# A fused linear-attention and FFN kernel on one Trainium2 core: another order of the same steps, with the front's large loads on SP's queue and other shares of DVE and ACT

## The chip, the cores and the metric

The kernel runs on one core of one Trainium2 chip. The metric is the device time of one execution in microseconds (us); the time before is 149.65 us, the median of three runs (149.62 to 149.75). The engines are named as in the profile: PE does the matrix products (PEld is its weight load), DVE, ACT and POOL work on vectors, and SP only issues transfers. ACT can issue transfers too. Each engine runs its own instruction list strictly in order, and engines wait for each other by semaphores.

## The reference

The input is one sequence of 2048 rows of 448 columns. The rows are normalised once, and two branches work on the result: an attention of 16 heads of 28 columns with a softmax feature map, and a two-layer FFN with a Mish activation. The output is the input plus both branches.

```
xn  = (x - mean) / sqrt(var + 1e-5)                     # per row
q, k, v = split heads of xn @ wqkv                      # 16 heads of 28
pq, pk  = q @ w_phi[h], k @ w_phi[h]
phi = concat(softmax(p), softmax(-p))                   # 56 features, for q and for k
kv, z   = sum_s phi_k x v, sum_s phi_k
o   = (phi_q @ kv) / (phi_q @ z + 1e-6)
A   = o @ wo
h   = xn @ w1 + b1;  B = (h * tanh(softplus(h))) @ w2   # Mish, 1792 wide
out = x + A + B
```

## The kernel before

The 2048 rows are 16 tiles t of 128 rows, or 8 pairs u of two tiles. The whole program is a list of named steps (ORDER, lines 181 to 198). `run_order` (L201) calls them one after the other; each step appends its instructions to the lists of the engines that it uses, and a resource tracker (class Program, L40) adds the semaphore waits that the data need. So the place of a name in ORDER sets its place on each engine that it uses, transfers included, and nothing else: two steps on different engines are ordered by data alone.

The names are built from a step, a tile, pair or part, and a last letter that says which engine does it: s SP, a ACT, d DVE, p POOL, m an SP transfer, b both ACT and DVE.

- **Loads.** `lx0` to `lx6` load rows of x (L307; lx0, lx1, lx2, lx3 two tiles each, from tile 0, 2, 4, 6; lx4 and lx6 four tiles each, from 8 and 12). `lkm` and `lvm` load the first 384 rows of the K and V weights into the tile Wkv (L310), `lkt` their last 64 rows twice, into both halves of the partitions (L315; `lktb` issues one copy on SP and one on ACT, `lkts` both on SP). `lp` is w_phi (tile Wraw, L330), `lb` is b1 (L334), `lqT0` to `lqT3` are transposing loads of the Q weight (L319), `l1m` and `l1t` load W1, `l2` W2, `lo` Wo. `table` loads ACT's function table (L348).
- **Row normalisation.** `st` computes mean and variance of one tile (two DVE instructions, L471 and L472, or five on ACT, L463 to L467). `rs` and `rt` compute 1/sqrt for a pair or for one tile (two on ACT, L483 and L485, or two on POOL, L477 and L480). `xn` and `xm` apply both (DVE L512, or after a shift on DVE, L490, on ACT L507 or on POOL L502). Pair 1 alone (tiles 2 and 3) goes by single tiles: `rt2`, `rt3`, `xm2`, `xm3`.
- **Transposes of the normalised rows** into xnT: `xt` for a pair, `xh` for one tile of pair 1. With a or d they go through PE (L520, L536) and are copied out by that engine (L527 or L525); with m they are an SP transfer (L546).
- **Folded weights.** `wtk0`, `wtk1` transpose the K weight on PE (L585) and copy it out; `bdp` builds the block-diagonal w_phi on POOL (tile Wbd, L568); `wmk0`, `wmk1` multiply the two (L609) into Wpk, `wmq0`, `wmq1` the same for Q into Wpq. `qd` (DVE, L323) doubles 64 columns of the transposed Q weight and needs all four `lqT`.
- **Products** (L433): `k`, `q`, `v` of a pair u and `f` of the FFN's first layer (f0.c and f1.c: half of the rows, column block c). Each product fills one of four pairs of PSUM banks and is cut in three parts, A, H and B, of 6, 2 and 6 matmuls of 64 partitions; two of these run at once, on the two halves of the array. The bank pair is taken at the first part and comes free when the evacuation is done: two exponentials on ACT for k (L650) and q (L712), a copy on ACT or DVE for v (L525 or L527), a Mish on ACT for f (L731).
- **The features of k.** `kn` sums over the features on DVE (L658, L660) and scales on POOL (L662), twice per pair u. `kv` accumulates phi_k times v on PE (L681), eight in all; `kvz` copies the sum out on DVE (L692) and turns it by an SP transfer (L698).
- **The end.** `e` turns the exponentials of q by an SP transfer (L720); `nd` forms numerator and denominator of a tile on PE (L754) and divides on DVE (L770 to L781), `ot` turns the result by an SP transfer (L789), `wo` multiplies by Wo (L877), `g` is the FFN's second layer (L860), the sum is added to x on DVE (L824) and stored (`sto`, L891). The last tile's last 64 columns come separately (L839 to L846, store L888).
- **Warm-up.** `z5` and `z6` are 5 and 6 matmuls on zeros (L402) at the head of PE's list; `b1` turns the bias on PE (L725) and DVE copies it out.

Four matters of this listing carry the steps below. PE's list begins z5, z6, b1, wtk0b, wtk1b, xh3d, xh2a, xt3a, wmk0a, wmk1b, and then the products. The copy of the K weight's tail that SP issues stands behind x's tiles 2, 3, 6 and 7 and w_phi. The engines' lists are in order, so a DVE instruction that waits holds all rows behind it. And the parts B and A of one product wait for each other on PE, so other products stand between them.

Of the kernel before, what the change touches and what calls it, by code (L numbers as in the profile page):

```python
# [178 lines left out]


ORDER = """
zero lx1s lx3s lba st2d lkma lps pw pp st6d lktb lx2s table z5 pi lvma st3a z6 pm lx4s rt3a st7d rs3a xm3a lqT0 rt2p
xm2d b1 xn3d wtk0b bdp wtk1b xh3d st5d xh2a st4d lqT2 xt3a wmk0a wmk1b lqT3 rs2p v1Aa lqT1 st8d v1Ha v3Bd lx6s st9a
v1Ba pk v3Hd k3B xn2d v3Ad rs4p qd k3H xt2m xn4d k3A st14d st15d st12d rs7p lx0s st11d k1H k1A wmq0a wmq1a k1B v2Bd
st13d k2A rs6a k2H v2Ad xn7p st10d q1H xt4m l1ms k2B xn6p v2Hd q1A q2B q1B q2H st1d st0d xt7m q2A e2 v4Ad rs5a v4Hd
k4A v4Bd k4H xn5d q3B k4B q3H q3A xt6m rs0p q4A v7Ha ep xn0d v7Aa kn2.0 xt5m kn4.0 e3 xt0m l1ts k7B v7Ba k7A k7H k6A
k6H pv kn3.0 v6Bd k6B q4B k5B v6Hd kn1.0 v6Ad k5H q4H v5Hd kn4.1 v5Ad k5A k0B kn7.1 v5Bd k0A k0H f0.1H kn3.1 f0.1A
f1.2A kn7.0 kn1.1 kn0.0 f0.1B f1.3H f1.3A f1.2H f0.0B f1.3B e9 e4 f1.0A kn2.1 f1.0H f0.0H kn6.0 f0.0A e7 f1.0B f1.2B
q7H e8 kn0.1 q7A q5A v0Hd q7B e5 e6 q5H v0Bd q6A los v0Ad q6H q5B q6B f1.9B kv3 kn5.1 kv4 kv7 e11 f0.7A f1.9H f1.9A
f0.7H f0.13A e10 f0.13H kv1 kv0 f0.13B e12 f0.7B e13 kn6.1 f1.13A f1.13H q0B f1.13B q0H f0.6H kn5.0 kv2 kv6 kv5 kvz  # L190
q0A f0.6A e1 f0.9H f0.9A f1.10A f1.10H f0.6B f0.2B f1.10B f0.2A f0.9B e14 f1.12A f0.2H e0 f1.11A f1.12H f0.5A f1.11H
nd1 f1.12B f1.11B f0.5B f1.8A f0.5H l2s nd2 f1.8H f0.8B f1.8B f0.10A nd3 ot1m f0.10H f0.8H f0.8A f1.5A f0.10B e15
f1.5B f1.1B nd0 f0.12H f1.1H f1.1A f0.12B f1.5H f0.3H f0.3A nd7 f0.3B f0.12A f1.7A ot0m f0.11B f1.7H f1.4B nd6 f1.7B
f1.4H ot3m f0.11H f1.4A f0.11A wo1H f0.4B f1.6B f0.4H f0.4A f1.6H nd10 f1.6A wo1B nd4 wo1A nd5 wob nd11 g3 g0 g2 ot2m
g1 nd13 wo3H wo3A wo0B nd12 ot5m wo3B wo0H ot6m nd14 sto1 wo0A g7 g6 g10 g11 nd8 wo5B nd15 ot7m wo5H nd9 wo5A sto3
wo2A g4 g5 g13 g12 ot4m g8 wo4B wo6H wo7A wo2H wo6A wo4H wo2B wo7B sto0 wo6B sto6 sto5 wo4A wo7H g9 g14 sto4 stt14
sto2 g15 stt15
"""


# [822 lines left out]
```

## Time and profile before

| | |
|---|---|
| median of three runs | 149.65 us |
| the profiled execution's own time | 149.63 us |
| its span in the trace | 147.4 us |
| PE busy | 143.1 us, 97% |
| DVE, ACT, POOL busy | 101.8, 77.0, 39.4 us |

The span is what the profiler sees from the first to the last instruction; the time of the execution lies 2.2 us above it. PE is busy in nearly all of the span: of the 40 slices of the page, the first two have 70%, the last 30%, and the others 90% or more. The chain of waits gives PE 93% of the span, DMA 4%, SP's queue and DVE 1% each. ACT is busy until 90 us, POOL until 56 us, DVE until the end.

### The profile page before, as it was taken

Reading aid. Unit: us, or ns where it says so; the run is one execution under the profiler, and the core shown is the slowest. Engines: PE = TensorE matmul, PEld = TensorE weight load, DVE = VectorE, ACT = ScalarE, POOL = GpSimd, SP = SyncE. Lnnn points to the kernel's source line nnn. Section 1 sums busy time; section 2 is a strip of 40 time slices with the busy share of each in tenths; the row PEclk is TensorE's granted clock in tenths of the full one; section 3 lists DMA queues with packets and bytes.
Section 4 is the critical chain, followed back from the end, with each engine's and each line's share of the span. In section 5 each row is a group of like instructions: output and inputs, shape, how many; then the busy total and the mean of one; then the engine's idle time right before and its main releaser. Section 6 shows DMA issues by size and latency. Waiting matters only on the chain.

```text
span 147.4 us, 3868 instructions
## 1 busy us (share of the span) xinstructions
PE 143.1 (97%) x1668; PEld 74.1 (50%) x1668; DVE 101.8 (69%) x227; ACT 77.0 (52%) x98; POOL 39.4 (27%) x54
## 2 busy tenths in 40 slices
PE   7799999999999999999999999999999999999993
PEld 2275555554445545444544446555555545547452
DVE  0898996989997921306999848998997499303522
ACT  3999999989889987996667575000000000000000
POOL 6334283399999990000000000000000000000000
PEclk9999999999999999999999999999999999999999
DMA  4995899995998195399707311015032004500313
GB/s 133 296 274 169 156 350 112 198 202 79 157 203 224 26 163 112 61 190 242 232 4 133 67 32 35 0 24 99 8 57 67 0 4 104 145 0 0 129 64 122
DMA packets 39964, 17.23 MB, mean 117 GB/s; under 512 B 33932, under 2 KB 39180, under 8 KB 39948
## 3 DMA queue, kind: packets, MB, share of 16 engines
q1 hardware_dynamic: 38896, 16.09, 51.3%
q10 hardware_dynamic: 1052, 0.91, 2.1%
q8 instruction: 13, 0.21, 0.6%
q14 instruction: 3, 0.02, 0.0%
HBM read 7.02 MB, written 1.84 MB: 60 GB/s over the span
## 4 chain that ended last, share of the span: by engine, by line
PE 93%; DMA 4%; SPq 1%; DVE 1%; issue 0%
PE PS L433 51%; PE PS L860 29%; PE PS L877 7%; DMA Wkv<-in_A_wqkv_dram 4%; PE PS L754 3%; PE PS L681 2%; PE PS L609 1%; SPq L307 1%; PE PS L585 0%; DVE x_all L824 0%; SPq L330 0%; PE PS L536 0%; PE PS L520 0%; DVE x_all L846 0%
## 5 line engine op out<-in xcount | busy, mean ns | idle before, releaser
L433 PE MATMUL PS<-xnT,W 64*128 64x512 bf16 x392 | 44.8, 376 | 0.0
L860 PE MATMUL PS<-W,actT 128*128 128x448 bf16 (+1 forms) x224 | 42.7, 351 | 0.0
L731 ACT ACTIVATE actT<-PS,b1T 128x1024 bf16<-128x1024 f32 x28 | 30.0, 1113 | 9.3 <-PE PS L433 9.2
L860 PEld LDWEIGHTS PS<-W,actT 128*128 128x128 bf16 x224 | 21.6, 98 | 20.6 <-issue 1.1
L433 PEld LDWEIGHTS PS<-xnT,W 64*128 64x128 bf16 x392 | 18.3, 94 | 21.0 <-issue 0.3
L662 POOL TENSOR_TENSOR actT<-actT,rSk 128x896 bf16<-128x896 bf16 x16 | 26.6, 1700 | 4.8 <-DVE rSk L660 4.8
L824 DVE TENSOR_TENSOR x_all<-PS,x_all 128x448 bf16<-128x448 f32 (+1 forms) x16 | 9.1, 614 | 13.9 <-PE PS L877 8.5
L658 DVE TENSOR_REDUCE Sk<-actT 128x32 f32<-128x896 bf16 x16 | 16.6, 1040 | 0.0
L650 ACT ACTIVATE actT<-PS 128x896 bf16<-128x896 f32 x16 | 13.8, 932 | 0.3 <-PE PS L433 0.2
L433 PE MATMUL PS<-Wkv,xnT 64*128 64x448 bf16 x112 | 13.2, 349 | 0.0
L770 DVE COPY Sq<-PS 128x16 f32<-128x16 f32 x32 | 4.0, 168 | 13.2 <-PE PS L754 13.2
L433 PE MATMUL PS<-Wpk,xnT 64*128 64x448 bf16 x112 | 13.1, 349 | 0.0
L433 PE MATMUL PS<-Wpq,xnT 64*128 64x448 bf16 x112 | 12.7, 349 | 0.0
L471 DVE BATCH_NORM_STATS2 stats<-x_all 128x6 f32<-128x448 bf16 x14 | 8.5, 606 | 3.5 <-DMA x_all<-in_A_x_dram 3.5
L778 DVE TENSOR_TENSOR v_all<-v_all 128x464 f32<-128x464 f32 x16 | 10.3, 643 | 0.6
L774 DVE TENSOR_TENSOR v_all<-PS,Sq 128x464 f32<-128x464 f32 x16 | 10.3, 641 | 0.5
L781 DVE TENSOR_TENSOR xn<-v_all,rden 128x448 bf16<-128x448 f32 x16 | 10.0, 625 | 0.6
L776 DVE TENSOR_TENSOR v_all<-PS,Sq 128x464 f32<-128x464 f32 x16 | 10.1, 630 | 0.0
L712 ACT ACTIVATE actT<-PS 128x896 bf16<-128x896 f32 x10 | 8.4, 925 | 0.6 <-PE PS L433 0.5
L527 DVE CAST v_all<-PS 128x896 bf16<-128x896 f32 x6 | 6.5, 1080 | 3.0 <-PE PS L433 3.0
L433 PEld LDWEIGHTS PS<-Wkv,xnT 64*128 64x128 bf16 x112 | 5.4, 94 | 5.0
L433 PEld LDWEIGHTS PS<-Wpq,xnT 64*128 64x128 bf16 x112 | 5.4, 94 | 5.1 <-ACT actT L731 0.2
(85 smaller groups left out, 121.0 us busy)
## 6 DMA issues: line engine op xcount, KB each, us to landing
W<-in_B_w_dram SPq DMA_DIRECT2D x1, 1568.0 KB, 8.2
out_dram<-x_all SPq DMA_DIRECT2D x7, 224.0 KB, 2.2
W<-in_B_w_dram SPq DMA_DIRECT2D x1, 1344.0 KB, 6.8
x_all<-in_A_x_dram SPq DMA_DIRECT2D x4, 224.0 KB, 2.9
x_all<-in_A_x_dram SPq DMA_DIRECT2D x2, 448.0 KB, 5.1
Wkv<-in_A_wqkv_dram ACTq DMA_DIRECT2D x2, 336.0 KB, 5.1
Wo<-in_A_wo_dram SPq DMA_DIRECT2D x2, 336.0 KB, 4.3
W<-in_B_w_dram SPq DMA_DIRECT2D x2, 224.0 KB, 3.6
```

Of the source, the lines that this page charges most:

```text
L433: ins = e.matmul(o, lhs(c, k), rhs(c, k), start=first and n == at[par][0], stop=last and n == at[par][-1])
L650: op("ACT", lambda e, s=s: e.activation(E_of(u)[:, s, :, :], two(b, D), ACT.Exp, scale=1.0 if s == 0 else -1.0), r=[pb(b), pb(b + 1)], w=[ ...
L658: op("DVE", lambda e: e.tensor_reduce(Sk[u][:, s, :], Eh(), AX.X, ALU.add), r=[("E", u, s)], w=[("Sk", u, s)], tag=f"Sk{u}.{s}")
L662: op("POOL", lambda e: e.tensor_tensor(Eh(), Eh(), ap_on(rSk[u][:, s, 0:1], [[1, 2 * H], [0, DH]]), ALU.mult), r=[("E", u, s), ("rSk", u, ...
L731: op("ACT", lambda e: e.activation(actT[:, fc, q * 1024:(q + 1) * 1024], bank(b, 2), ACT.Mish, bias=b1T[:, fc:fc + 1]), r=[("b1T",), pb(b) ...
L774: op("DVE", lambda e: e.tensor_tensor(tv(t1[i]), num(0), sx(1), ALU.mult), r=[pb(b), pb(b + 1), ("Sq", i, 1)], w=[("t1", i)], tag=f"ta{t}")
L776: op("DVE", lambda e: e.tensor_tensor(tv(t2), num(1), sx(0), ALU.mult), r=[pb(b), pb(b + 1), ("Sq", i, 0)], w=[("t2",)], tag=f"tb{t}")
L778: op("DVE", lambda e: e.tensor_tensor(t1[i], t1[i], t2, ALU.add), r=[("t1", i), ("t2",)], w=[("t1", i)], tag=f"tc{t}")
L781: op("DVE", lambda e: e.tensor_tensor(o_sb[(t // 2) % 2][:, t % 2, :].rearrange("p (h d) -> p h d", d=DH), t1[i][:, :, 0:DH], ap_on(rden[i ...
L824: op("DVE", lambda e: e.tensor_tensor(x_all[:, t, 0:n], bank(b)[:, 0:n], x_all[:, t, 0:n], ALU.add), r=[pb(b), ("x", t)], w=[("out", t)], ...
L860: ins = e.matmul(bank(b)[:, 0:width(t)], actT[:, fc, tok(t)], W2[:, fc, 0:width(t)], start=first and fc == 0, stop=last and fc == FC - 1)
L877: ins = e.matmul(bank(b)[:, 0:w], oT_of(u)[lo:hi, cc * P:(cc + 1) * P], Wo[lo:hi, cc, 0:w], start=first and n == at[par][0], stop=last and ...
```

## The change

Only ORDER changes; no function does. The new list has as many steps as the old, and 30 of them carry another letter or count. In words:

- **Loads.** `lkma`, `lktb`, `lvma` become `lkms`, `lkts`, `lvms`: the K and V weights are issued on SP. SP's list now begins lx3, lx1, lp, lkm, lkt (two copies), lx2, lvm, lx4, lx6, lqT0, lqT3, lqT1, lqT2, xt2m, lx0, l1m, xt4m, xt5m, xt7m, xt0m, xt6m, l1t (two). Before it began lx1, lx3, lp, lkt (one copy), lx2, lx4, lqT0, lqT2, lqT3, lqT1, lx6, xt2m, lx0, xt4m, l1m, xt7m. ACT's list begins with `table`, and then the one small load lb.
- **First rows.** Statistics: tiles 7, 3, 2 on DVE and tile 6 on ACT (before: 2, 6, 7 on DVE, 3 on ACT). `rs3`, `rt2`, `rt3` all on ACT (before, rt2 on POOL). `xn3`, `xm2`, `xm3` all on DVE (before, xm3 on ACT with its shift on DVE). `xh2` and `xh3` both copied out by DVE (before, xh2 by ACT). `wtk1` copied out by ACT alone (before by both), `wmk0` by both (before by ACT), `wmq0` by DVE (before by ACT).
- **Later rows.** `st9` on DVE and `st11` on ACT (before the other way round); `rs5` and `rs6` on POOL (before on ACT); `xn7` on DVE (before on POOL). v2, v3, v4 and v0 are copied out by ACT (before by DVE). `pv`, a memset on POOL, moves ahead of the `kn` rows, `pk` behind them.
- **Warm-up.** z10, b1, z4 in place of z5, z6, b1: 14 matmuls on zeros, four of them behind b1.
- **Order of the products.** After v1, v3, k1, k3 come k2, v2, q1, q2, q3, k4, v4, k5, v5, k7, k0, v0, v7, k6, four f, then q5, q4, v6, q6. The `kv` steps stand earlier, the `nd` steps begin with nd3, nd2, and the list ends g8, g9, g5, g4, g15 (before wo4A, wo7H, g9, g14, g15).

```diff
--- before.py
+++ after.py
@@ -179,22 +179,21 @@
 ORDER = """
-zero lx1s lx3s lba st2d lkma lps pw pp st6d lktb lx2s table z5 pi lvma st3a z6 pm lx4s rt3a st7d rs3a xm3a lqT0 rt2p
-xm2d b1 xn3d wtk0b bdp wtk1b xh3d st5d xh2a st4d lqT2 xt3a wmk0a wmk1b lqT3 rs2p v1Aa lqT1 st8d v1Ha v3Bd lx6s st9a
-v1Ba pk v3Hd k3B xn2d v3Ad rs4p qd k3H xt2m xn4d k3A st14d st15d st12d rs7p lx0s st11d k1H k1A wmq0a wmq1a k1B v2Bd
-st13d k2A rs6a k2H v2Ad xn7p st10d q1H xt4m l1ms k2B xn6p v2Hd q1A q2B q1B q2H st1d st0d xt7m q2A e2 v4Ad rs5a v4Hd
-k4A v4Bd k4H xn5d q3B k4B q3H q3A xt6m rs0p q4A v7Ha ep xn0d v7Aa kn2.0 xt5m kn4.0 e3 xt0m l1ts k7B v7Ba k7A k7H k6A
-k6H pv kn3.0 v6Bd k6B q4B k5B v6Hd kn1.0 v6Ad k5H q4H v5Hd kn4.1 v5Ad k5A k0B kn7.1 v5Bd k0A k0H f0.1H kn3.1 f0.1A
...
-f1.5B f1.1B nd0 f0.12H f1.1H f1.1A f0.12B f1.5H f0.3H f0.3A nd7 f0.3B f0.12A f1.7A ot0m f0.11B f1.7H f1.4B nd6 f1.7B
-f1.4H ot3m f0.11H f1.4A f0.11A wo1H f0.4B f1.6B f0.4H f0.4A f1.6H nd10 f1.6A wo1B nd4 wo1A nd5 wob nd11 g3 g0 g2 ot2m
-g1 nd13 wo3H wo3A wo0B nd12 ot5m wo3B wo0H ot6m nd14 sto1 wo0A g7 g6 g10 g11 nd8 wo5B nd15 ot7m wo5H nd9 wo5A sto3
-wo2A g4 g5 g13 g12 ot4m g8 wo4B wo6H wo7A wo2H wo6A wo4H wo2B wo7B sto0 wo6B sto6 sto5 wo4A wo7H g9 g14 sto4 stt14
-sto2 g15 stt15
+zero table lx3s lba pi st7d st6a lx1s pp st3d lps st2d rs3a rt2a z10 pw rt3a lkms lkts lx2s pm b1 xn3d lvms xm2d lx4s
+xm3d z4 wtk0b bdp wtk1a xh2d xh3d st4d st5d xt3a wmk0b lx6s wmk1b rs2p v1Ha lqT0 v3Ba lqT3 v1Ba st11a lqT1 xn2d v3Aa
+v3Ha k3H k1B lqT2 v1Aa st8d xt2m ep st9d k1H k1A qd st10d k3A wmq0d rs4p wmq1a pv k3B k2A k2H lx0s st15d l1ms v2Ha q1B
+xn4d k2B st14d rs5p rs7p st1d q1H v2Ba q1A xt4m q2H xn5d v2Aa xn7d q3H q2A xt5m q3A q2B st0d st12d q3B k4B xt7m v4Ba
+rs0p k4A st13d k4H rs6p k5B xn0d xn6p v4Aa xt0m kn1.1 k5H xt6m v5Ad kn2.1 v4Ha v5Hd k5A kn3.1 v5Bd k7H k7A k0B k7B
+v0Ba v7Ha k0H l1ts v0Ha k0A v7Ba k6B e2 e5 v7Aa k6H kn4.1 k6A f1.2A v0Aa f1.2H f1.3B f1.2B kn3.0 los f1.0A f0.1A f1.0H
+kn4.0 e3 f0.1H kn0.1 kn5.1 f1.3H kn1.0 kn5.0 f1.3A kn7.1 f0.1B e6 q5B kn2.0 f1.0B e4 q4B v6Bd q4A v6Hd kn6.1 e7 q4H
+q6B v6Ad q5A q5H q6A kv1 kv3 q6H f1.7B f1.11A kn0.0 e8 f1.7A kn6.0 f1.11H f1.7H f0.7B kv5 kv2 kv4 f1.11B kn7.0 f0.7A
+f1.9B f0.7H f0.10B kv6 kv0 kv7 f1.9H pk e13 kvz f1.9A e12 f0.6H f0.10A f0.10H f0.6A f0.0B f0.6B f0.0H f0.0A q7A e9 q0A
+q0H q7H e10 nd3 q0B f1.12B e0 q7B f1.12H f1.8H f1.8A e11 nd2 f1.8B f1.12A f0.13A f0.13H f1.10B f0.13B f1.10A f0.8A
+ot1m f1.10H f1.5B nd6 f0.8H f1.5A e1 f0.3H f1.5H f0.3A f0.8B nd7 e15 f0.5B f0.3B f0.5H f0.11B f0.5A nd0 f1.6H f1.6A
...
+f1.4H f0.4B f1.4B f0.9B f0.4H f0.12B nd13 f0.4A f0.9H f0.9A wo0B nd11 wo0A wo0H nd12 nd10 ot6m g1 g0 g12 g13 nd5 wo1H
+wo1A wo6H wo6A ot5m nd4 wo1B nd15 wo6B g2 g6 ot2m g3 wo3H nd9 sto6 nd14 wo3B nd8 wo3A g7 ot7m g10 ot4m g11 g14 wo2A
+wo4H wo7B sto3 wob wo4B wo5H wo2H wo7A wo4A wo5B wo2B wo7H sto0 sto1 wo5A g8 g9 sto4 g5 g4 stt14 sto5 sto2 g15 stt15
 """
```

More of the change, by code (lines that the diff above doesn't have):

```diff
@@ L187 @@
-k6H pv kn3.0 v6Bd k6B q4B k5B v6Hd kn1.0 v6Ad k5H q4H v5Hd kn4.1 v5Ad k5A k0B kn7.1 v5Bd k0A k0H f0.1H kn3.1 f0.1A
[L188 to L191, printed above, removed]
```

2 lines of the change are left out of this document (1 added, 1 removed).

## The prediction

> **What bounds the kernel now.** I read the page's shares first, then the chain of waits in order of time (start, length, what).
>
> ```profile
> PE 143.1 (97%) x1668; PEld 74.1 (50%) x1668; DVE 101.8 (69%) x227; ACT 77.0 (52%) x98; POOL 39.4 (27%) x54
> ```
>
> ```profile
> 2.20 5.20 DMA Wkv<-in_A_wqkv_dram
> ...
> 7.44 0.65 PE PS L585 x8
> 8.10 0.39 PE PS L536 x7
> 8.49 0.39 PE PS L520 x7
> 8.88 0.79 PE PS L609 x16
> 9.67 4.84 PE PS L433 x50
> 14.50 0.89 PE PS L609 x16
> 15.40 34.03 PE PS L433 x348
> ...
> 57.50 0.88 PE PS L681 x96
> ...
> 144.45 0.56 DVE x_all L824
> ```
>
> The reader is to see three stretches. Until 7.40 the chain is the second copy of the K weight's tail, issued by SP at 2.20. Until 9.67 it is PE with little rows in a fixed order. From 9.67 to 144.4 it is PE alone. The same matmuls are done after the change, and both lists end with g15, its DVE sum and the stores, so the 2.97 us from 144.43 to the span's end stay, and the 2.23 us between span (147.4) and time (149.63) too. What can change is **when the products start**, and **whether PE, in its new order, is ever made to wait**. The profiled run stands 0.02 under the median of 149.65; I count against the median, with 0.2% (0.3 us) as what a measurement can tell from no change.
>
> **The front: loads.** The timeline of the first microseconds (start, length, engine, line):
>
> ```profile
> 0.82 0.87 SPq L307 DMA_DIRECT2D x_all<-in_A_x_dram  x2
> 0.96 4.87 PE L402 MATMUL PS<-zeros 128*128 128x512 bf16 x11 [0.96 <-POOL zeros L354]
> 2.20 0.55 SPq L315 DMA_DIRECT2D Wkv<-in_A_wqkv_dram  x1
> 2.51 1.28 ACT L348 ACT_TABLE_LOAD   x1 [2.51 <-issue]
> 3.47 0.63 DVE L471 BATCH_NORM_STATS2 stats<-x_all 128x6 f32<-128x448 bf16 x1 [3.47 <-DMA x_all<-in_A_x_dram]
> 3.80 0.58 ACT L463 ACTIVATE junk<-x_all 128x448 bf16<-128x448 bf16 x1
> 3.90 5.21 SPq L319 DMA_TRANSPOSE WqT<-in_A_wqkv_dram  x4
> 5.53 0.30 ACT L483 ACTIVATE lnv<-mv,eps_col 128x1 f32<-128x1 f32 x1
> 6.56 1.14 DVE L512 TENSOR_SCALAR xn<-x_all,mv,rstd 128x448 bf16<-128x448 bf16 x3
> 6.98 1.13 POOL L568 TENSOR_TENSOR Wbd<-Wraw,mask 112x224 bf16<-112x224 bf16 x2 [1.67 <-DMA Wraw<-in_A_w_phi_dram]
> ```
>
> SP issues about every 0.5 us. In the new list the K weight goes out at 2.2 and its tails at 2.65 and 3.2, before x's tiles 4 and 5 and the V weight instead of beside them. Up to and with the second tail that is 224+224+24.5+336+112+112 = 1032 KB, 1057 thousand bytes. The table of stages (last column GB/s) says when so much had flowed before:
>
> ```profile
> 0.00:5.00 5.00, 4.04 (x10) 1.50 (x11) 1.46 (x5) 2.42 (x5) 3.03 (x18) 1.00 0.63 181
> 5.00:6.20 1.20, 0.95 (x4) 0.10 (x2) 0.86 (x5) 1.14 (x5) 0.31 (x1) 1.00 1.03 235
> 6.20:7.40 1.20, 0.65 (x8) 0.50 (x8) 1.20 (x6) 1.17 (x5) 0.42 (x1) 1.00 1.07 332
> ```
>
> 905 thousand by 5.0, the other 152 at 235 GB/s by 5.65. With 0.4 to 0.9 for the slowest engine and the completion the tails land at 6.0 to 6.6 instead of 7.40. The opposite bound is that landing follows issue: 3.2 + 5.2 = 8.4. I take the first, since by 7.40 some 1585 thousand bytes had flowed (905 + 282 + 398, the last at 332 GB/s), half as many again as these need; the second is a rival below. The Trainium skill's page "DMA: Bandwidth & Descriptors", section "Issuing engines are not separate DMA queues", speaks against the change: transfers of all issuers run on the same 16 engines, and a second issuer saves just the issue time. By that the move gives nothing back for the last tail's 1.0 us later issue; the bytes ahead of it, which the change does cut, are what that sentence leaves out.
>
> **The front: DVE, ACT, PE.** The table load now starts at 0.8 and is over at 2.1, so ACT's statistics start with x at 3.47, not at 3.80. They took 1.73 to the first L483 (3.80 to 5.53), so rs3 stands from 5.20 to 5.73; rt2 waits for DVE's third statistics, whose place and end (5.79) are unchanged, and ends at 6.35, rt3 at 6.8. DVE's prices:
>
> ```profile
> 10.28 0.59 DVE L527 CAST Wpk<-PS 128x448 bf16<-128x448 f32 x1
> 10.79 0.62 DVE L471 BATCH_NORM_STATS2 stats<-x_all 128x6 f32<-128x448 bf16 x1
> 14.12 0.22 DVE L323 COPY WqT<-WqT 128x256 bf16<-128x256 bf16 x1
> 14.25 0.89 DVE L512 TENSOR_SCALAR xn<-x_all,mv,rstd 128x448 bf16<-128x448 bf16 x3
> 15.05 0.62 DVE L471 BATCH_NORM_STATS2 stats<-x_all 128x6 f32<-128x448 bf16 x1
> 15.80 0.59 DVE L471 BATCH_NORM_STATS2 stats<-x_all 128x6 f32<-128x448 bf16 x1
> ```
>
> A pair of normalised tiles takes 0.80 (14.25 to 15.05), or 1.06 beside POOL's L568 as at 6.56; one tile's statistics 0.75 (15.05 to 15.80), a copy of half of Wpk 0.51 (10.28 to 10.79). From 5.80: bias 0.1, xn3 0.8, xm2 0.3, xm3 0.5, and 0 to 0.25 for POOL's L568, which falls beside them: done at 7.6 to 7.85. The copies for wtk0, xh2, xh3 (384 or 512 columns; 0.35 to 0.4 each, an estimate from the 0.22 of L323's 256) end at 8.6 to 8.9.
>
> PE: 11 warm-ups took 4.87, some 0.43 apart, so z10 ends at 5.3; b1; then z4. b1 now holds z4 and all behind it until the bias has landed; before, it was used at 5.8, right after the warm-ups, so at worst it is 0.4 late, and I take 0. Later 512-wide matmuls stream twice as fast:
>
> ```profile
> L433 PE MATMUL PS<-xnT,W 64*128 64x512 bf16 x392 | 44.8, 376 | 0.0
> ```
>
> (two run at once: 44.8 over 196 is 0.23). z4 costs 1.7 at the slow rate, ending at 7.1, or 1.1 with one slow and three fast, ending at 6.5. I take 6.5, since the 8 matmuls of L585 at 6.19 in the trace ran fast (0.65 for 8 against 0.43 for one warm-up). The page "TensorE: Matmul & The Clock Gate" of the skill, Part 1, says that the clock doubles after about 4 us of activity, give or take half a microsecond from run to run; by it the new front would differ between runs by up to 0.7, which the three runs of before (149.62 to 149.75) don't show, though there the K weight at 7.40 could hide it. The granted clock of the stages reads 1.00 throughout and doesn't show this doubling.
>
> So wtk0 runs 6.5 to 6.95 (8 at the 0.056 of L536's 7 in 0.39), wtk1 to 7.4 (tails landed), xh2 to 7.6, xh3 waits for xm3 and ends at 7.85 to 8.1, xt3 at 8.25 to 8.5, wmk0 and wmk1 (0.79, their copies done by 8.65) at 9.05 to 9.3. v1's part H, two matmuls, follows, then v3B waits for ACT's copies of wtk1 and xt3 (1024 and 896 columns, some 0.9 each by the row of L712 below, after 7.6: 9.5). **v3B starts at 9.55** (9.3 to 9.85) with 2 of the first 50 matmuls done. At 4.84/50 = 0.097 that is 0.3 ahead of the 9.67 of before; bounds 0 ahead and 0.55 ahead.
>
> **To wmq0.** The other 48 last 4.6: PE is there at 14.15. But wmq0 needs `qd`, and DVE's list ahead of it is, from 8.75: st4, st5 (1.5), two copies of Wpk (1.0), xn2 (0.8), st8 (0.75), ep (0.35, an estimate for three small instructions), st9 (0.75), qd (0.2): 14.1, up to 14.4. The four lqT, 1.30 of issue each (5.21 for 4) behind lx6 from 6.2, end their issue at 11.4 and land near 13. So wmq0 starts at 14.1 to 14.4 where the chain had 14.50: **0.25 gained**.
>
> **After that PE must stay full.** These are the points where a bank pair, a transfer or POOL could be late. ACT's and POOL's prices and W1's load:
>
> ```profile
> 20.86 3.34 ACT L712 ACTIVATE actT<-PS 128x896 bf16<-128x896 f32 x4
> 24.05 0.34 ACT L483 ACTIVATE lnv<-mv,eps_col 128x2 f32<-128x2 f32 x1
> ```
>
> ```profile
> 18.95 3.46 POOL L502 TENSOR_SCALAR xn<-x_all,rstd,shift 128x448 bf16<-128x448 bf16 x6 [1.24 <-DVE shift L490]
> 28.15 3.35 POOL L662 TENSOR_TENSOR actT<-actT,rSk 128x896 bf16<-128x896 bf16 x2 [4.76 <-DVE rSk L660]
> 31.85 23.34 POOL L662 TENSOR_TENSOR actT<-actT,rSk 128x896 bf16<-128x896 bf16 x14
> ```
>
> ```profile
> W<-in_B_w_dram SPq DMA_DIRECT2D x1, 1344.0 KB, 6.8
> ```
>
> - ACT takes four more copies of v (0.8 each, as 20.86 to 24.05 is 0.8 per instruction), +3.2, and sheds wmq0 and four small rows, about 1.7; k6, k0 and q4 stand elsewhere. A pair of exponentials takes 1.6. From wmq0 at 14.25: wmq1's copy ends at 16.25, k3's exponentials at 17.85, k2's (k2 ready at 18.0) at 19.6, and q3, which takes k2's banks, is due on PE after wmq (0.89) and 50 matmuls (4.7) at 19.9. Slack 0.3. The next such places (k5 behind q2, v5 behind q3, v0 behind k5) have 0.3 to 0.7. If ACT is slower than that, the cost is the excess, at most the 1.5 of net load.
> - W1 now goes out ahead of xt4: SP's xt2 waits for xn2 at 12.1, its issue takes 1.3 and lx0's and W1's 0.6 each, so W1 is issued at 14.3 and lands 6.8 later at 21.1, xt4 behind it at 21.6. k4 is due after wmq and 76 matmuls (7.2) at 22.3. Slack 0.7.
> - POOL's 16 scalings take 23.34/14 = 1.67 each, 26.7 in all. After qd DVE has seven statistics (5.2), two copies of Wpq (1.0) and four pairs (3.2) ahead of POOL's xn6: 23.8. xn6 is half of 3.46, so the first scaling starts at 25.6, not 28.15, and the last ends at 52.3. PE reaches kv7, which needs it, after 308 matmuls of 448 columns (at 0.0945, from the 34.03 of the chain), 110 of 512 (0.108), wmq (0.89) and seven kv (0.29 each, 0.88/3): 9.36 + 43.9 = 53.3. Slack 1.0; before it was 2.3 (57.50 against 55.19).
> - The later nd, e and wo steps I counted only roughly, and found some tenths to spare; I take 0, and up to 0.3 if one is late.
>
> Sum: -0.25, other stretches 0: **149.4**.
>
> **Rivals.** (1) *The front gains more*: z4 fast throughout, L568 not beside DVE's rows, qd at 13.95: 0.4 to 0.8 with the few tenths that PE loses inside its 34 us. For it: every term above is at its middle; against: qd's list. 149.0. (2) *No gain*: z4 slow moves all of PE's small rows by 0.6, to wtk1 at 8.0 and v3B at 9.95, or DVE reaches qd late. For it: DVE took on xm3 and a copy. 149.7. (3) *A wait takes the gain back*, the slower side: POOL's last scaling. It decides when the first scaling starts later than 26.6; each microsecond later is one on PE, which has nothing else in order. Started at 28.15, as before, it ends at 54.85 and costs 1.55. For it: DVE's list holds seven statistics that wait for x and for POOL's own small rows; against: the count above. 149.9 to 150.9, centre 150.3; ACT's bank pairs give the like. (4) *Landing follows issue*: tails at 8.4, wtk1 to 8.85, ACT's two copies to 10.8, v3B there: 1.05 late, 150.7. Against: the bytes. That the loads would not go where the diff says is no rival: ORDER sets the queue.
>
> **How the numbers follow.** Forecast (149.2 to 149.6) 0.44; (1) 0.22; (2) 0.12; (3) 0.15; (4) 0.07. Faster by over 0.3: (1) and two fifths of the forecast, 0.40. Within 0.3: the rest of the forecast and most of (2), 0.36. Slower: (3), (4) and the rest of (2), 0.24. The range 148.9 to 150.4 leaves out the far ends of (1), (3) and (4).
>
> **What would show it.** In the changed trace: L585's second group at 6.9 rather than 7.44; the first L433 on Wkv near 9.1 and the next part near 9.55; the second L609 group at 14.1 to 14.4; W1 landed by 21.5; the first L662 near 25.6; no idle on PE between. A PE wait on L662, on L650 or on xnT would make the forecast wrong upward; a start of L433 before 9.0, downward.

## The result, and the profile after

The changed kernel takes **151.57 us** (median of 4, 151.27 to 152.35) against 149.70 for the kernel before on the same chip (149.62 to 150.17): ratio 1.0126, interval 1.0083 to 1.017. The forecast was 149.4, the range 148.9 to 150.4; the time lies above its upper end. A second set of runs (a0 below) gives 151.81 against 149.89, ratio 1.0127 (1.0087 to 1.0166). Times and ratios leave out executions that are over 1.5% above the fastest of the same kernel; the profiles of h1 and b2 are of such executions and are not used.

The profiled execution of the changed kernel took 151.27 with a span of 148.8; before it was 149.63 with 147.4. Lines of the changed kernel stand one lower than before (L585 is L584, L609 L608, L433 L432, L681 L680, L754 L753). The page's engine shares after:

```profile
PE 144.6 (97%) x1671; PEld 76.3 (51%) x1671; DVE 100.5 (68%) x229; ACT 78.2 (53%) x95; POOL 38.6 (26%) x53
```

PE is still busy for 97%, and nothing in this line tells why the kernel is slower. The chain of waits after, in order of time (start, length, what):

```profile
2.19 4.77 DMA Wkv<-in_A_wqkv_dram
...
7.01 1.24 PE PS L584 x16
8.25 0.39 PE PS L535 x7
8.64 0.39 PE PS L519 x7
9.03 0.90 PE PS L608 x16
9.93 4.95 PE PS L432 x50
14.88 0.89 PE PS L608 x16
15.78 30.49 PE PS L432 x312
46.27 0.61 PE PS L680 x64
46.88 3.41 PE PS L432 x30
50.29 1.05 PE PS L680 x96
51.33 2.91 PE PS L432 x26
54.25 0.94 PE PS L680 x96
...
57.07 1.23 SPq L697
...
58.34 1.34 SPq L719
...
59.72 3.39 DMA EqT<-actT
...
63.14 1.66 ACT Eq L711 x2
...
64.84 0.40 PE PS L753 x16
65.24 5.72 PE PS L432 x52
```

Before, the chain reached PE at 7.44 and stayed on it until the last sum. Now it leaves PE again between 55 and 65: kvz on DVE, then SP's issue of kvT (L697), then SP's issue of e12 (L719) behind it, the transfer, the two exponentials of q0 that write where e12 reads, and at last nd2, which waits for them to free q0's bank. The timeline has the wait on PE (last column: idle time and its releaser):

```profile
7.01 1.24 PE L584 MATMUL PS<-ident,Wkv 128*112 128x128 bf16 x16 [0.51 <-DMA Wkv<-in_A_wqkv_dram]
...
9.86 1.43 PE L432 MATMUL PS<-Wkv,xnT 64*128 64x448 bf16 x12
...
64.84 0.40 PE L753 MATMUL PS<-KVZ,EqT 56*128 56x60 bf16 x16 [0.26 <-ACT Eq L711]
```

The 1.64 us between the two profiled executions divide as follows.

| where | before | after | difference |
|---|---|---|---|
| up to the start of wmq0 (chain) | 14.50 | 14.88 | 0.38 |
| nd2: idle 0.26, and 0.40 for what takes 0.22 elsewhere | 0 | 0.44 | 0.44 |
| kv groups (chain: 0.61, 1.05, 0.94; before 0.61, 0.88, 0.88) | 2.37 | 2.60 | 0.23 |
| small waits of PE, 0.04 to 0.12 each (what is left of the span's 1.4) | | | 0.35 |
| time outside the span | 2.23 | 2.47 | 0.24 |

The first row can be read off the two chains: L535 begins 0.15 later than L536 did (8.25, 8.10), the L608 group takes 0.11 longer (0.90, 0.79) and the first 50 products 0.11 longer (4.95, 4.84). The 0.15 is the K weight's. The other two are waits for ACT, which now copies all of wtk1 and then xt3:

```profile
7.76 1.55 ACT L524 ACTIVATE Eq<-PS 112x512 bf16<-112x512 bf16 x2 [1.07 <-PE PS L584]
9.21 0.91 ACT L524 ACTIVATE xnT<-PS 128x896 bf16<-128x896 bf16 x1
10.17 1.63 PEld L432 LDWEIGHTS PS<-Wkv,xnT 64*128 64x128 bf16 x20 [0.21 <-ACT xnT L524]
```

The copy of wtk1 ends at 9.31, and the matmuls of wmk1, which read it, begin at 9.36; the copy of xt3 ends at 10.12, and v3B begins at 10.17.

The row of small waits is a remainder, but the trace shows where it lies: PE is held by 0.12 at 16.40, 0.08 at 47.74, 0.09 at 66.46 and 0.04 at 70.90, and each time what its weight load waited for last is an instruction on ACT (L649, L711, L711, L730).

The front has moved later, not earlier. Its loads, by the table of stages (length, busy times, clock, DMA share, GB/s), first before, then after:

```profile
2.50:3.50 1.00, 1.00 (x3) 0.30 (x2) 0.03 (x1) 0.99 (x1) 0.67 (x4) 1.00 1.00 344
3.50:4.50 1.00, 1.00 (x4) 0.45 (x3) 0.97 (x3) 0.96 (x3) 0.15 (x2) 1.00 1.11 355
```

```profile
2.50:3.50 1.00, 1.00 (x4) 0.29 (x2) 0.10 (x1) 0.10 (x1) 0.86 (x5) 1.00 1.03 375
3.50:4.50 1.00, 1.00 (x4) 0.44 (x3) 0.97 (x3) 0.94 (x4) 0.06 (x1) 1.00 0.66 83
```

and SP's issues after:

```profile
2.19 0.49 SPq L309 DMA_DIRECT2D Wkv<-in_A_wqkv_dram  x1
2.73 1.20 SPq L314 DMA_DIRECT2D Wkv<-in_A_wqkv_dram  x2
```

At first both move much the same (344 and 375 GB/s), then the new stream has a hole of a microsecond at 83 GB/s where the old one ran at 355. Before, ACT issued the main part of the K weight at 1.52 and one tail at 1.95; now SP issues the main part at 2.19 and the tails at 2.73 and 3.33.

### The profile page after: what moved, and what is told of

It reads as the page before. It is cut to its first block, busy times and chain, and to the rows that moved or that the text cites. A ratio compares the mean times of both kernels' runs of the same rounds, so it can differ in the third digit from the quotient of the medians.

```text
span 148.8 us, 3871 instructions
## 1 busy us (share of the span) xinstructions
PE 144.6 (97%) x1671; PEld 76.3 (51%) x1671; DVE 100.5 (68%) x229; ACT 78.2 (53%) x95; POOL 38.6 (26%) x53
## 4 chain that ended last, share of the span: by engine, by line
PE 87%; DMA 5%; SPq 3%; DVE 2%; ACT 1%; issue 0%; ACTq 0%
PE PS L432 44%; PE PS L859 29%; PE PS L876 7%; DMA Wkv<-in_A_wqkv_dram 3%; PE PS L753 3%; DMA EqT<-actT 2%; PE PS L680 2%; DVE KVT L691 1%; PE PS L608 1%; ACT Eq L711 1%; SPq L719 1%; PE PS L584 1%; SPq L697 1%; SPq L306 1%; DVE x_all L823 0%
## 5 line engine op out<-in xcount | busy, mean ns | idle before, releaser
L432 PE MATMUL PS<-xnT,W 64*128 64x512 bf16 x392 | 44.9, 376 | 0.0
L730 ACT ACTIVATE actT<-PS,b1T 128x1024 bf16<-128x1024 f32 x28 | 30.3, 1113 | 9.2 <-PE PS L432 9.2
L432 PEld LDWEIGHTS PS<-xnT,W 64*128 64x128 bf16 x392 | 18.8, 94 | 20.9 <-ACT actT L711 0.8
L661 POOL TENSOR_TENSOR actT<-actT,rSk 128x896 bf16<-128x896 bf16 x16 | 26.5, 1695 | 0.0
L823 DVE TENSOR_TENSOR x_all<-PS,x_all 128x448 bf16<-128x448 f32 (+1 forms) x16 | 9.4, 615 | 16.5 <-PE PS L859 9.6
L649 ACT ACTIVATE actT<-PS 128x896 bf16<-128x896 f32 x16 | 14.1, 955 | 0.4 <-PE PS L432 0.3
L432 PE MATMUL PS<-Wkv,xnT 64*128 64x448 bf16 x112 | 13.7, 349 | 0.0
L432 PE MATMUL PS<-Wpk,xnT 64*128 64x448 bf16 x112 | 13.0, 349 | 0.0
L432 PE MATMUL PS<-Wpq,xnT 64*128 64x448 bf16 x112 | 12.9, 349 | 0.0
L711 ACT ACTIVATE actT<-PS 128x896 bf16<-128x896 f32 x10 | 8.6, 936 | 0.0
L432 PEld LDWEIGHTS PS<-Wpq,xnT 64*128 64x128 bf16 x112 | 6.0, 94 | 4.5 <-ACT actT L649 0.2
L432 PEld LDWEIGHTS PS<-Wpk,xnT 64*128 64x128 bf16 x112 | 6.0, 94 | 4.5 <-ACT actT L649 0.4
L432 PEld LDWEIGHTS PS<-Wkv,xnT 64*128 64x128 bf16 x112 | 5.9, 94 | 4.8 <-ACT actT L649 0.2
```

Source lines behind the costliest of these rows:

```text
L432: ins = e.matmul(o, lhs(c, k), rhs(c, k), start=first and n == at[par][0], stop=last and n == at[par][-1])
L649: op("ACT", lambda e, s=s: e.activation(E_of(u)[:, s, :, :], two(b, D), ACT.Exp, scale=1.0 if s == 0 else -1.0), r=[pb(b), pb(b + 1)], w=[ ...
L661: op("POOL", lambda e: e.tensor_tensor(Eh(), Eh(), ap_on(rSk[u][:, s, 0:1], [[1, 2 * H], [0, DH]]), ALU.mult), r=[("E", u, s), ("rSk", u, ...
L711: op("ACT", lambda e, s=s: e.activation(Eq_of(u)[:, :, s, :].rearrange("p i (h n) -> p i h n", n=64)[:, :, :, 0:QP], two(b, D).rearrange(" ...
L730: op("ACT", lambda e: e.activation(actT[:, fc, q * 1024:(q + 1) * 1024], bank(b, 2), ACT.Mish, bias=b1T[:, fc:fc + 1]), r=[("b1T",), pb(b) ...
```

## The experiments

Theory: three separate losses, the front (K's landing), e12 behind kvT, and W1 ahead of x4's transpose. Rivals: the new shares of DVE and ACT set the front; the later order loses in many small places. All edits are to ORDER alone, and each ratio is to the kernel before, timed beside it on the same chip.

**a0: the changed kernel again** (no edit).

> The changed kernel once more, unedited, for a second trace and its spread beside the others. If the loss lies in fixed places (front +0.5 us, the wait of nd2 for q0's exponentials +0.4, small ones +0.5 against before), the second trace shows the same places and some 151.5 us. If the loss is a matter of chance (landing times), the places differ between the two traces.

151.81 us, ratio 1.0127 (1.0087 to 1.0166). In the profile nd2 waits again (0.38 at 65.0), the first product starts at 10.11, the span is 149.0. The losses are in the same places; the front stands 0.25 later.

### The front

**e1: K's and V's weights on ACT's queue again.**

```diff
-zero table lx3s lba pi st7d st6a lx1s
+zero lx3s lba lkma pi st7d lx1s
...
-lps
-lkms lkts
-lvms
+lps lktb table lvma st6a
```

> The K and V weights back on ACT's queue with the table load behind K's tail, all else as changed. If the loads on one queue are what delays the front, the first matmuls on Wkv start at 9.6 or earlier (9.86 changed) and the time falls by 0.3 to 0.5 against the changed kernel. If ACT's own larger share in the first rows (all of wtk1's copy, then xt3's) is what delays it, the start of v3B stays near 10.1 and the time within 0.2.

The front missed: K's last tail was issued at 2.20, as before, and landed at 8.23, so that the first product came at 10.55. 151.39, ratio 1.0093 (1.0062 to 1.0124); of the 0.42 below a0's median, 0.25 lies outside the span (2.17 to 2.26 here). The timeline of PE:

```profile
6.52 0.65 PE L584 MATMUL PS<-ident,Wkv 128*112 128x128 bf16 x8 [0.22 <-DMA Wkv<-in_A_wqkv_dram]
8.28 0.65 PE L584 MATMUL PS<-ident,Wkv 128*112 128x128 bf16 x8 [1.11 <-DMA Wkv<-in_A_wqkv_dram]
```

The second group is the one that needs the tails: it starts at 8.28, where before's stood at 7.44. An early issue alone doesn't bring the tail early, nor does a fuller stream: from 3.5 to 4.5 it carried 287 GB/s here, where the changed kernel's had 83.

**e2: w_phi behind K's tails** (`lps` moved behind `lkts`).

> w_phi is issued behind the K weight and its tails on SP, all else as changed. If w_phi's 56-byte pieces make the hole in the single queue's stream (58 and 106 GB/s between 3.5 and 4.5 us), the K weight is whole at 6.0 to 6.4 instead of 6.96, L584 starts when z4 ends (6.5), and the time falls by 0.2 to 0.5. If the K weight is late because it is issued in series on one queue, L584 starts at 6.8 or later and the time changes by less than 0.15.

151.60, ratio 1.011 (1.0082 to 1.0137). The stream from 3.5 to 4.5 ran at 157 GB/s, the second group started at 7.80. w_phi's small pieces are not what makes the K weight late, and the hole is still there without them.

**e4: only the loads of the change, and the table's place, in the order of before.**

```diff
-zero lx1s lx3s lba st2d lkma lps pw pp st6d lktb lx2s table z5 pi lvma st3a z6 pm lx4s rt3a
+zero table lx1s lx3s lba st2d lps lkms lkts pw pp st6d lx2s lvms z5 pi st3a z6 pm lx4s lx6s rt3a
```

> The kernel before with only the loads changed: both K and V weight loads on SP in the changed kernel's order (w_phi, K main, K tails, x2, V, x4, x6), the table ahead of b1's load on ACT; shares of DVE and ACT, products and all later steps as before. Theory A (one queue's stream has a hole that ACT's loads filled, so the K weight is whole about 0.4 to 0.5 later on PE): the bytes moved from 3.5 to 4.5 us fall to 200 GB/s or less, the second transposition of the K weight starts at 7.8 to 8.1 in place of 7.44, the first product follows 0.3 to 0.5 later than before's 9.67 and the time is 150.1 to 150.4. Rival (the front's lateness comes from the new shares of DVE and ACT): the transposition starts at 7.44 or earlier and the time is 149.5 to 149.9.

151.33, from 150.14 to 152.22, ratio 1.0082 (1.0031 to 1.0133). The stream from 3.5 to 4.5 fell to 107 GB/s, so the new loads alone make the hole. In the profile the second group started at 7.74, a little ahead of the forecast, but then PE ran at half its pace:

```profile
7.74 0.70 PE L585 MATMUL PS<-ident,Wkv 128*112 128x128 bf16 x8 [0.26 <-DMA Wkv<-in_A_wqkv_dram]
8.24 0.95 PE L536 MATMUL PS<-ident,xn 128*128 128x128 bf16 x7
8.99 0.95 PE L520 MATMUL PS<-ident,xn 128*128 128x128 bf16 x7
9.73 1.70 PE L609 MATMUL PS<-Wbd,Eq 112*128 112x112 bf16 x16
11.36 1.99 PE L433 MATMUL PS<-Wkv,xnT 64*128 64x448 bf16 x18
```

L536's seven begin 0.75 ahead of the next row here (8.24 to 8.99); in before's chain they took 0.39. So the first product came at 11.36. The table of stages shows why (the third number from the end is the granted clock):

```profile
8.20:11.40 3.20, 3.20 (x36) 3.03 (x35) 2.26 (x6) 2.51 (x4) 0.42 (x2) 0.50 1.53 325
```

The granted clock was 0.50. The seven times fall into two groups by it: three executions with a mean clock of 0.989, as in this profile, took 151.73 to 152.22, and four with 1.000 took 150.14 to 151.33. These four measure the loads without the slow PE. Their spans have a median of 148.2, against 147.7 for the kernel before beside them, and they leave 2.43 to 2.51 outside. So the new loads alone cost about 0.5 in the span, as theory A has it, and 0.24 outside it. Four executions that spread by 1.2 make this a rough size.

**h1 and r1: hybrids.** h1 has before's order up to `k1B` and then the changed order of what is left; r1 has the changed order up to `qd` and then before's.

> A hybrid: the order of before from its first step up to the product k1B (the whole front: loads on SP's and ACT's queues, table behind the tails, first rows on DVE and ACT as before), then every step that is left in the changed kernel's order. If the front and the table's place are the larger part of the loss (0.5 in the span, 0.24 outside), the time is 150.9 to 151.2, with W1 ahead of x4's transpose perhaps taking 0.2 to 0.4 of it back at k4. If the loss lies in the later order (kv part, nd2 and the small waits), the time is 151.4 to 151.8.

> The other hybrid: the changed kernel's order from its first step up to qd (the whole new front), then every step that is left in the order of before. If the front and the table's place are the larger part of the loss, the time is 150.5 to 150.8 (before's 149.9 and 0.6 to 0.9); if it lies in the later order, 150.0 to 150.3. The two hybrids' losses should add up to that of the whole change, 1.9.

h1: 150.82, ratio 1.0078 (1.0046 to 1.0111). r1: 151.78, ratio 1.0123 (1.0087 to 1.016). The two losses against 149.78, 1.04 and 2.00, don't add up to 1.9, so the hybrids don't split the change: in r1 the copies that the changed order had given to ACT met the copies that before's order gives to ACT. The waits of PE in r1, by engine and line:

```profile
PE PS L433 <- ACT actT L650: 0.6, 1, 0.6
...
PE PS L433 <- ACT Wpq L525: 0.2, 1, 0.2
```

What h1 shows is that with before's front a loss of 1 us remains. In the span it is even 1.4 (149.0 against 147.6), for h1 has only 1.75 to 1.86 outside the span where the kernel before has 2.18 to 2.28.

**b0 and b1: the kernel before once more, and with w_phi behind K's tail** (`lps` behind `lktb`).

> The kernel before itself, for a second trace of its front: the second transposition of the K weight starts between 7.1 and 7.9 (7.44 in the profile shown, 7.84 with the same loads in h2), the first product 2.2 later, the time 149.4 to 150.3.

> The kernel before with w_phi's load behind K's second tail on SP, so that this tail is issued at 1.74 in place of 2.20; nothing else is changed. Theory A (the front hangs on the issue of K's tails): the second transposition starts 0.2 to 0.4 sooner, at 7.0 to 7.2, and the time is 0.1 to 0.4 lower, 149.5 to 149.9 against before's 149.9 to 150.0. Rival (bytes ahead and beside set it, of which w_phi has 24.5 KB): 7.4 to 7.8 as in before, no change of the time.

b0: 149.74. The second group started at 6.66, 0.78 sooner than in the profile shown, the first product at 9.24, and the span is 147.5, no shorter. The chain of b0 shows who took it back:

```profile
20.34 5.37 DMA xnT<-xn
...
25.84 4.32 PE PS L433 x43
```

x7's transpose, issued behind W1's load, landed at 25.7. In this trace the order of before had no use for an early front either. In b1 (150.12, ratio 1.0007, 0.9982 to 1.0032) the tails landed early too, but w_phi was late for POOL, and wmk0 waited for POOL:

```profile
9.28 0.96 PE L609 MATMUL PS<-Wbd,Eq 112*128 112x112 bf16 x16 [0.86 <-POOL Wbd L568]
```

### e12, W1 and what stands behind it

**e3: e12 and e9 ahead of kvz's transfer on SP.**

```diff
-pk e13 kvz f1.9A e12 f0.6H
+pk e13 e12 e9 kvz f1.9A f0.6H
...
-q7A e9 q0A
+q7A q0A
```

> e12 and e9 go ahead of the transfer of kvz on SP, all else as changed. If nd2 waits because e12, q0's exponentials behind it and so nd2's banks stand behind SP's wait for kvz, the 0.42 us that PE lost at nd2 go and the time falls by 0.3 to 0.5. If something else would be late there instead (q0's exponentials held by ACT's own list), the time stays within 0.15.

151.27, ratio 1.0091 (1.006 to 1.0122), 0.54 below a0 of the same rounds, whose interval overlaps. In the trace the wait at nd2 is gone, as expected. The front of this run was early (first product 9.60), and that gain was lost in a new place, the first part of k4:

```profile
17.87 5.12 DMA xnT<-xn
...
23.12 6.97 PE PS L432 x71
```

x4's transpose, issued at 17.87 behind W1's load (15.01), took 5.12. It held PE up by 0.47.

**e6: e3 with W1's load behind x4's transpose** (`l1ms` behind `xt4m`).

> The changed kernel with e12 and e9 ahead of kvz on SP (as in e3_e12_first) and, new, W1's load (l1ms) behind the transpose of x4 (xt4m) on SP. In e3 the front was early (wmq0 at 14.55) and 0.47 us of it were lost again at k4, which waited for x4's transpose behind W1's bytes. Theory A (W1 ahead of x4 is what gives an early front back): PE waits neither at k4 nor at nd2, W1 lands about 1 us later and its first reader still finds it, and the time is 0.3 to 0.5 below e3's, 150.8 to 151.0. Rival (k4 is late for another reason, its V or K copies on ACT): the wait at k4 stays at 0.2 to 0.5 and the time is e3's 151.3.

Far off: 155.41, ratio 1.0351 (1.0308 to 1.0394). k4 no longer waited; k5 did, 2.6 us:

```profile
20.84 6.93 DMA xnT<-xn
27.91 23.04 PE PS L432 x216
```

W1 was issued at 19.88, and x5's transpose at 20.84 landed 6.93 later, nearly W1's own time (issue to landing 7.0). Behind this wait the granted clock was 0.50 from 28.2 to 31.6, so 3.4 us passed at half pace, which is some 1.7 of PE's work; the wait alone is not the whole loss.

**e8: x4 early, its transpose ahead of W1** (`rs4p` behind `st9d`, `xn4d` behind `wmq0d`, `st10d` behind it, `xt4m` ahead of `l1ms`, and e3's edit).

> The changed kernel with e12 and e9 ahead of kvz on SP, and x4 made early as in the order of before: rs4 and xn4 ahead of st10 on POOL and DVE, x4's transpose ahead of W1's load on SP. Nothing of the front up to the first products is touched. Theory A (W1 ahead of x4 costs up to 0.5 at k4, and in e6 the same wait only moved to x5 since W1 was issued 5 us later): W1 is issued near 16.5, PE waits neither for x4 nor for x5 by more than 0.1, nor at nd2, and the time is 151.0 to 151.3, 0.5 to 0.8 below the changed kernel's 151.8. Rival (some wait always takes its place, x5 now): 151.3 to 151.8 with a wait of 0.3 or more at k5.

The premise failed. `xn4` still stood behind qd and wmq0's copies on DVE, so x4's transpose went out at 18.02 and W1 at 19.29, not at 16.5. 152.96, ratio 1.0209 (1.0177 to 1.0241), and k5 waited 1.5:

```profile
21.73 5.04 DMA xnT<-xn
...
26.90 3.18 PE PS L433 x31
```

**e11: e3 with W1's load straight behind x2's transpose, ahead of x0's load** (`l1ms` behind `xt2m`).

> e3_e12_first with W1's load straight behind x2's transpose on SP, ahead of x0's load: issued about 0.9 us sooner (near 14.1) with nothing else moved. In e6 and e8 W1 was issued at 19.9 and 19.3 and k5 waited 2.6 and 1.5 us for x5's transpose behind it; in e3 at 15.0 and k4 waited 0.47 for x4's. Theory A (a transpose lands when the bytes issued ahead of it have landed): W1 lands near 21.1, x4 near 21.9, the waits at k4 and k5 are under 0.1, and the time is 0.3 to 0.5 below e3's 151.27 where the front is as early as e3's: 150.8 to 151.0. Rival (k4 waits for something else): a wait of 0.3 to 0.5 stays at k4 when the front is early.

153.89, ratio 1.0256 (1.0212 to 1.03), where e3 had 1.0091. x4 was in time, but x0's load now stood behind W1, and DVE's list behind it:

```profile
15.21 6.79 DMA x_all<-in_A_x_dram
...
22.03 0.64 DVE stats L470
```

DVE's statistics of tile 1 waited until 22.03, x5's rows came after them, and k5 waited 2.1 us for x5's transpose.

**e12: e11 with the K and V loads on ACT, x6 behind the Q weight's transposes.**

> e11_w1_sooner with K's and V's weight loads on ACT's queue again (the table behind K's tail) as in e1, and x6's load behind the transposes of the Q weight as in the order of before. In e1 K's last tail was issued at 2.20 and landed only at 8.24, with x4 and x6 issued by 4.5. Theory A (what is issued beside the tails delays them: bytes): with x6 out of the way the second transposition starts at 7.3 to 7.7, the first product follows at 9.6 to 10.0, the time is 150.2 to 150.7. Rival (issue or queue alone sets it, or chance): it starts at 8.0 or later as in e1, and the time is that of e11 or above.

The second group started at 7.71, against 8.28 in e1 and 7.53 in e11, and the first product at 10.07. With x6 out of the way the tail came sooner than in e1, as theory A has it, but no sooner than from SP. 153.50, ratio 1.0246 (1.0197 to 1.0295), with e11's wait at k5.

**e13: e3 with x0's load ahead of x2's transpose and W1 straight behind that** (`lx0s` ahead of `xt2m`, `l1ms` behind it).

> e3_e12_first with x0's load ahead of x2's transpose on SP and W1's load straight behind that transpose: W1 is issued 0.4 to 0.6 us sooner than in e3 (15.0), and x0's load, the victim of e11, stands ahead of it. Theory A (only what is issued behind W1 is late): DVE has no stall for x0, x4's transpose lands 0.4 to 0.5 sooner after the front's start than in e3, the wait at k4 falls from 0.47 to under 0.15 where the front is as early, no wait at k5, and the time is 0.1 to 0.4 below e3's 151.27. Rival (the first transposes suffer from x0's load beside them): x2's transpose lands later, k2 waits, and the time is e3's or more.

The profile went as theory A says: W1 issued at 14.19, no wait at k4, k5 or nd2. The chain is PE alone from the end of wmq0 to the first kv group; its row there:

```profile
15.98 14.10 PE PS L432 x147
```

The time didn't follow in full: 151.64, ratio 1.0107 (1.0084 to 1.013), no better than e3's within the intervals. The profiled execution has a span of 148.5 with a first product at 10.06; the median span of the six is 149.2.

**h2: h1 with e3's edit and x4's transpose ahead of W1.**

> The hybrid h1 (front of before up to k1B, then the changed kernel's order) with the two late waits taken out: e12 and e9 ahead of kvz on SP, and x4's transpose ahead of W1's load. h1's loss against before was 0.8% (1.05 us). If that loss is k4's wait behind W1 and nd2's wait (0.3 to 0.5 each), the time is 0.7 to 1.0 below h1's 150.9: 149.9 to 150.2, and PE waits at neither place. If the later order loses in many small places, it is 150.4 to 150.8.

150.43, ratio 1.0048 (1.0022 to 1.0074) against h1's 1.0078: about a third of the loss is gone, and the rest is as the second case has it. Its profile has no wait at nd2, but 0.33 at k5 for x5's transpose behind W1 and 0.46 at 17.7 for ACT's copy of wmq.

### The time outside the span

**e7: the table behind the two first issues. a10: the table's load four times more at the end** (`table` behind `lba`; `table` four times behind `wob`).

> The changed kernel with the exponential table's load on ACT behind the load issues lx3s and lba in place of ahead of them. The time outside the profiled span was 2.44 to 2.49 in every profiled execution of an order that begins with the table, and 2.17 to 2.24 where the loads go ahead of it. Theory A (the place of the table sets it): outside the span 2.17 to 2.24 again, x3 lands earlier against the span's start or the same, and the time is 0.1 to 0.3 lower than the changed kernel's, 151.5 to 151.7. Rival (the difference is only where the span is counted from: what leaves the outside goes into the span): the outside falls to 2.2 and the span grows by as much, same time, 151.8.

> The changed kernel with the table's load repeated four times at the end, where ACT has no work left (behind wob): four more instructions of ACT and nothing else. The time outside the profiled span was 2.41 to 2.52 in every execution of an order with 110 instructions on ACT and 2.16 to 2.28 in every one with 113 to 118, wherever the table stood (e7). If the number of ACT's instructions goes with it, the outside falls to 2.2 here and the time is about 0.2 lower, 151.5 to 151.6. If it does not, the outside stays at 2.45 and the time at 151.8.

e7: 151.70, ratio 1.0113 (1.0077 to 1.0149), 2.45 to 2.50 outside the span. a10: 152.13, ratio 1.0151 (1.0124 to 1.0178), 2.40 to 2.47 outside. The table's place doesn't set it. a10's trace has only one more instruction on ACT, so it puts the count to no test; e4, with 115 on ACT and 2.41 to 2.52 outside, contradicts it. These two runs are of more use for the front. Their first products:

```profile
10.54 0.67 PE L432 MATMUL PS<-Wkv,xnT 64*128 64x448 bf16 x4
```

```profile
10.77 0.36 PE L433 MATMUL PS<-Wkv,xnT 64*128 64x448 bf16 x2
```

### A version faster than both

**b2: the kernel before with x7's rows normalised by DVE** (`xn7p` becomes `xn7d`).

> The kernel before with x7's rows normalised by DVE in place of POOL: POOL's three pieces started at 18.58 behind a shift that stands in DVE's list behind the statistics of x5 and x6, DVE's own need no shift. Theory A (x7's transpose behind W1 is what caps an early front in the order of before): x7's transpose is issued about 1 us sooner (19.3), the wait at 25.8 goes, and the time is 0.1 to 0.3 below before's 149.9 to 150.1. Rival (DVE is the tighter engine there: the V copy of x2 behind it comes 0.7 later and holds PE's banks): PE waits 0.2 to 0.7 near 20 and the time is 150.0 to 150.6.

149.45, ratio 0.9974 (0.9955 to 0.9992): faster than the kernel before by 0.1 to 0.5%. About half lies in the span (median 147.5 against 147.8 of the kernel before beside it) and half outside it (1.91 against 2.22). No trace shows whether x7's wait is gone.

## Why the prediction was wrong

**The front: K's landing (first step that failed).** The prediction had the tails at 6.0 to 6.6 by counting bytes, the second group of L585 at 6.9, the first product near 9.1. In the changed kernel the main part of the K weight landed at 6.96 and the tails at 7.30 and 7.55; the second group started at 7.59 and the first product at 9.86. In ten other profiles of the new loads (a0, e2, e3, e6, e7, e8, e11, e13, r1, a10) the first product lies at 9.60 to 10.77. The bytes ahead of the tails were counted rightly, and so was the pace of the old stream; wrong was to give that pace to a stream issued by one engine, and to take the tails as landed when the bytes up to them have flowed. By 5.0 the table of stages has 136 GB/s after, where the sum used 181 of before:

```profile
0.00:5.00 5.00, 4.04 (x10) 1.31 (x10) 1.53 (x5) 2.82 (x6) 2.53 (x16) 1.00 0.49 136
```

680 thousand bytes instead of 905. With the pace that was (305 GB/s from 5.0 to 6.0, then 235) the 1057 thousand had flowed at 6.3, not 5.65, which is most of the error; the 0.4 to 0.9 that the sum adds for the slowest engine and the completion comes from no row, and here 1.2 passed from 6.3 to the last tail. The loads that had filled the gap were the ones that ACT issued 0.7 to 0.8 sooner. e4 shows that the new order of the loads makes the hole, with before's shares of DVE and ACT. That the hole alone makes the tails late is not shown: in e1 the early issue came back, by 5.0 the stream had 173 GB/s, and the last tail landed at 8.23 all the same, with x4 and x6 issued beside it; e12, with x6 later, had it 0.56 sooner. The forecast's opposite bound, issue plus 5.2, or 8.4, was as far off on the other side for the profiled execution, yet is near a10's. The rule that the prediction quoted of the Trainium skill's page "DMA: Bandwidth & Descriptors", section "Issuing engines are not separate DMA queues", fits e12 beside e11: the last tail, issued 1.1 sooner with K's other parts on ACT's queue, landed at 7.67 against 7.49, no sooner, though x6's load had been moved out of its way as well.

**The front: DVE, ACT, PE (right in size, but not free).** z4 ended near 6.5 as taken. From the second group's start to the first product it is 2.27 in every profile with the changed front and loads but one (e2, with w_phi late, 2.37), against 2.16 before. The prediction had 2.15 (6.95 to 9.1). The 0.11 is the wait for ACT's copy of wtk1, and v3B waited 0.12 for ACT's copy of xt3, as forecast, though less: it began 0.31 after the first product, and the forecast had 0.45. So against the kernel before the new shares of ACT cost 0.22 of the front's 0.38 in the profiled pair, and the K weight 0.15; against the forecast nearly all of the error is the K weight (second group 7.59 for 6.95). The profiled pair shows little of what the loads do: the last tail landed at 6.61 to 7.79 in four traces with before's loads (before, b0, h2, and b1 with w_phi moved) and at 7.28 to 8.46 in twelve with the new ones (e4 and the eleven above). Where K came early with before's loads, the rows of x showed too: in b0 the stretch took 2.58, and PE waited 0.2 for ACT's rows.

**To wmq0.** Forecast 14.1 to 14.4, measured 14.82, or 14.88 in the chain; qd ended at 14.70. The forecast took qd as the bound; with the late front PE comes later than qd, if only by 0.1. The error is 0.6, and 0.64 of lateness was there already at the second group (7.59 for 6.95).

**Slack of x4 behind W1, 0.7 (used up).** The order of events was right: W1 issued at 14.96 (forecast 14.3), landed 7.0 later at 21.98 (21.1), x4 behind it, and k4's parts at 22.86 with no wait above 0.02. But the 0.7 existed only against a PE that is itself late. When the front was early (e3), k4 waited 0.47. In no trace here did a transfer issued behind W1 land ahead of it, and W1 took 6.0 to 7.1 us. So x4 (e3), x5 (e6, e8) and x0 (e11) each paid in turn; in before it is x7 (b0). In the two traces with an early front (e3, b0) this wait took 0.47 and 0.34 back, which the sum did not see.

**"The later nd, e and wo steps I counted only roughly; I take 0" (second step that failed).** This is the largest single term after wmq0. e12's issue stands behind kvT on SP, kvT behind kvz, and kvz behind the last kv group; q0's exponentials wait for e12, nd2 for q0's bank. Forecast 0 to 0.3, measured 0.44; e3 moves two names and the wait is gone. The prediction followed SP's queue where W1 passes x4's transpose, but not at 57 us, where kvz's transfer passes e12.

**POOL's last scaling (right).** The rival had it at 1.55. The first scaling began at 26.60 (forecast 25.6) and the last ended at 53.12, 1.06 ahead of the last kv group at 54.18 (forecast slack 1.0), and no row of PE waits for L661. The 0.23 by which the kv groups run longer shows in no row as a wait for these scalings; what makes it isn't known. ACT's bank pairs, the other half of this rival, cost no more than 0.12 in any one place, nd2 aside.

**The time outside the span (third step that failed).** It was carried over as 2.23. It is 2.44 to 2.49 in every execution of the changed kernel and 2.15 to 2.28 in every one of the kernel before beside the experiments: 0.24 of the loss, from no place in the trace.

**Sum.** Forecast -0.25, measured +1.64 in the profiled executions. The difference of 1.89 is 0.63 at wmq0, 0.24 outside the span, and 1.02 behind wmq0: 0.44 at nd2, 0.23 in the kv groups and some 0.35 in waits of 0.12 or less behind ACT that were taken as 0 and that no run separates. The profiles bear this out as a whole. Span less first product is 138.9 to 139.1 in five profiles with the wait at nd2 (changed 148.8 less 9.86, a0 149.0 less 10.11, e2 149.2 less 10.17, e7 149.6 less 10.54, a10 149.8 less 10.77), so there a late K weight goes into the time one for one. It is 138.4 in e13, which has neither nd2's nor k4's wait, and 137.8 before (138.3 in b0, with x7's wait). Of the 1.1 to 1.3 behind the first product, then, 0.5 to 0.7 goes with nd2's wait; the remaining 0.6 is in the kv groups and the small waits.

**Open.** What in the new order of the loads opens the hole in the stream, and what else sets the tails' landing; the 0.6 of kv groups and small waits; what sets the time outside the span; and why e13's median does not show the 0.5 that its profile does. So that the wait at nd2 is gone with e12's move is shown by e3's and e13's traces; that the whole time falls by as much is not shown.

## What to carry to other kernels

Before forecasting what a change of one stage is worth, look for the next transfer that ties the engines together again: in these runs the large load held everything issued behind it on its queue until it had landed, so moving it mostly chose another victim, and an earlier front ended at that point. Follow each transfer that is moved to every queue it passes, late in the program as well, and look for an operation whose buffer it frees. The pace of a stream belongs to the order in which its pieces were issued, so bytes divided by the old pace are at best a lower bound for a new order. And before a run's time is set aside, look at the granted clock of each execution: in e4 it separates the loads' cost from the slow PE's.
